# Gated mix of linear attention and a dense layer on one core: the first token tile loaded in two halves, other first loads in changed places, and parts of the first projection, the outputs and the last tile in another order

## The chip, the cores and the metric

The kernel runs on one core of one Trainium2 chip. A core has five engines with an instruction queue each: TensorE (PE) for matmuls, VectorE (DVE), ScalarE (ACT), GpSimd (POOL) and SyncE (SP), and 16 DMA engines that all queues feed. PE reads SBUF and writes PSUM; DVE and ACT bring results from PSUM back to SBUF. DMAs are issued here from SP and from ACT. The metric is the device time of the whole launch in microseconds, median over several runs.

## The reference

2048 tokens of width 512 go through two branches, mixed by a gate per token. Cut to what matters:

```
x: 2048 x 512; H = 32 heads of 16; wqkv 512 x 1536; w1 512 x 1376; w2 1376 x 512
g   = sigmoid((x * gate_w).sum(-1))
q, k, v = heads of x @ wqkv
phi(t)  = concat(softmax(t @ w_phi), softmax(-t @ w_phi))     # per head, 32 features
kv  = sum over tokens of phi(k)^T v;   z = sum over tokens of phi(k)
o   = (phi(q) @ kv) / (phi(q) @ z + 1e-6)
a   = o @ wo
b   = relu(x @ w1) @ w2
out = g * a + (1 - g) * b                                      # bf16
```

## The kernel before

The kernel is written as a graph of named tasks. Each task belongs to one engine, has the tasks it depends on, and becomes a few instructions; the dependences become semaphore waits. The order of the tasks on each engine is not computed: it is written out by hand in the table `ORDER` (`sp`, `pool`, `act`, `dve`, `pe`), and each engine runs its list strictly in that order. An engine whose next task waits holds up everything behind it. The tokens are cut into 16 tiles of 128 (number `m`) and 4 chunks of 512.

*Start.* PE first runs `warm0`: six matmuls of constants, 128x512, that need no load (L258). The first chunk of x comes as four plain loads `x00` to `x03` (one tile each, 128 KB), the first 512 columns of `w1` as four loads `w1a0` to `w1a3` (128 KB each, one per 128 rows), all at L272. ACT issues `x01`, `w1a1`, `w1a3`; SP issues `x00`, `w1a0`, `w1a2`, `x02`, `x03`, and after them `w1b` (512 KB), `wphi`, `wkT`, `w1c`, `wv`, the other chunks of x (`x1` to `x3`, transposed by the DMA, L277), `wqT` and the rest. Each tile of the first chunk is transposed on PE: `xt{m}0` and `xt{m}1`, two matmuls of 128 columns each against an identity (L350), and `xe{m}0` on ACT (L362) and `xe{m}1` on DVE (L365) bring the two halves to SBUF. `xt20` to `xt31` reuse the PSUM banks of tiles 0 and 1. Then comes the first layer, `h`: for the first tiles in pieces, `hh00` (tile 0, needs `xe00` and `w1a0`), `hh01` (tile 1, needs `xe10`), `hh1`, `hh2`, `hh3` (L405; they need `w1a1`, `w1a2`, `w1a3`), `hr0`, `hr1`, `h0_0` to `h0_3` (L411), and whole ones after that (L391), with a relu on ACT each (`rl`, L469).

*Middle.* The heads' `w_phi` is folded into the projections: `f1_0` to `f1_3` (L374) make the key matrix `WP` in four blocks of 128 rows, which `fe1_0`, `fe1_2` (DVE, L344) and `fe1_1`, `fe1_3` (ACT, L342) evict. `pr_k0` to `pr_k8` and `pr_q0` to `pr_q8` (L512) multiply one or two token tiles with it, four matmuls a tile; `pr_k0` is the first, for tiles 0 and 1. Each projection goes through an eviction on ACT (`ev`, L539), minima and maxima on DVE (`mn`, `mx`), shifts on POOL (`t1`, `t2`, L552), an exponential on ACT (`ex`, L557), sums and reciprocals on DVE (`sm`, `rc`), and a product on POOL (`nm`). Key tiles are summed on PE into `kv` (L573); query tiles are transposed by a DMA from SP (`tq`, L592).

*Outputs.* For each tile, PE makes numerators and denominators, `nd{m}_0` and `nd{m}_1` (L616); DVE divides (`rd`, `o`, L623 and L625); a DMA from SP transposes the result (`to{m}`, L630). `b{m}` is eleven matmuls of the relu layer against `w2` (L638) into one of four PSUM banks, and `a{m}` four more of the attention branch against `wo` (L644) on top of it in the same bank; a bank is free again when the tile four before has been evicted. `oe{m}` on ACT (L689) multiplies by one minus the gate into one of five output buffers, and `st{m}` (L692), issued on ACT, stores 128 KB.

*Last tile.* Tile 15 is cut into columns 0 to 352 and 352 to 512, in two banks: `b15` (L659, 22 matmuls for both parts), then `a15_0` and `a15_1` (L670). `oe15_0` runs on ACT (L677) and is stored from ACT, `oe15_1` on DVE (L680) and stored from SP (L683). SP then waits for the last stores.

Of the kernel before, what the change touches and what calls it, by code (L numbers as in the profile page):

```python
# [5 lines left out]
ACT = mybir.ActivationFunctionType  # L6
ALU = mybir.AluOpType
# [14 lines left out]
    ),  # L22
# [6 lines left out]
    "act": (  # L29
# [8 lines left out]
    ),  # L38
    "dve": (
# [10 lines left out]
    ),  # L50
# [10 lines left out]
    ),  # L61
# [87 lines left out]
def bass_gated_mix__linear_kernel_hedgehog__dense_activation_relu__prompt_kernel(  # L149
# [11 lines left out]
    x2 = A_x.rearrange("b s d -> (b s) d")  # L161
    o2 = out.rearrange("b s d -> (b s) d")
    S, D = x2.shape
    H, DH = A_w_phi.shape[0], A_w_phi.shape[1]
    DFF = B_w1.shape[1]
    P = 128
    NT = S // P
    ND = D // P
    NC = S // 512
    KT = (DFF + P - 1) // P  # L170
# [10 lines left out]
    NPH, NOM, NOT, NOS = 7, 3, 4, 5  # L181
    NDB, AB = (6, 7), (3, 4, 5, 2)
    GATE_LIMIT = 40.0
    WARM = (6 * (512,),)
    RL = 400.0
    FE = "dve"

    with ExitStack() as es:
# [5 lines left out]
        XT = sb("XT", [P, ND, S], BF16)  # L194
        HT = sb("HT", [P, KT, S], BF16)
        WT = sb("WT", [P, 2 * ND, D], BF16)
        WP = sb("WP", [P, 2, ND, D], BF16)
# [13 lines left out]
        OSB = sb("OSB", [P, NOS, D], BF16)  # L211
# [19 lines left out]
        OMG = sb("OMG", [P, NT], FP32)  # L231
        PS = E(nc.psum_tensor("PS", [P, 8, 512], FP32))
# [5 lines left out]
        def psap(off, dims):  # L238
            return ap(PS, EPS, off, dims)

        g = _Graph()
        add = g.add
# [5 lines left out]
            boost=700.0)  # L248
# [22 lines left out]
        def load(name, eng, out_, in_, deps=(), dur=0.1, lat=6.0, **how):  # L271
            add(name, eng, lambda q: q.dma_start(out=out_, in_=in_, **how), deps, dur=dur, lat=lat, dma=True,  # L272
                boost=1e4)
            after_last(name, eng)
# [12 lines left out]
        def load_x(m, eng, lat):  # L287
            load(f"x0{m}", eng, XN[:, m, :], x0r[:, m, :], dur=0.45, lat=lat)

        def load_w(j, eng, lat):  # L290
            load(f"w1a{j}", eng, W1[:, j, 0:512], w1r[:, j, 0:512], dur=0.45, lat=lat)

        load_x(0, "sp", 2.95)
        load_x(1, "act", 3.1)
        load_w(0, "sp", 3.2)
        load_w(1, "act", 3.4)
        load_w(2, "sp", 3.8)
        load_w(3, "act", 3.95)
        load_x(2, "sp", 4.0)
# [54 lines left out]
        for m in range(4):  # L354
            for n in range(2):
                add(f"xt{m}{n}", "pe", lambda q, m=m, n=n: pe_xt(q, m, n),
                    (f"x0{m}", "ident", f"xe{m - 2}{n}" if m > 1 else None), dur=0.2, boost=9000.0 - 10 * m)
            for n, eng in enumerate(("act", "dve")):
                xo = XT[:, 2 * n:2 * n + 2, m * P:(m + 1) * P]
                xi = PS[:, XB[m][n], 0:2 * P].rearrange("p (j t) -> p j t", j=2)  # L360
                if eng == "act":
                    add(f"xe{m}{n}", eng, lambda q, o=xo, i=xi: q.activation(o, i, ACT.Copy), (f"xt{m}{n}",), dur=0.35,  # L362
                        boost=9000.0 - 10 * m)
                else:
                    add(f"xe{m}{n}", eng, lambda q, o=xo, i=xi: q.tensor_copy(o, i), (f"xt{m}{n}",), dur=0.37,  # L365
                        boost=9000.0 - 10 * m)
        x0 = [f"xe{m}{n}" for m in range(4) for n in range(2)]
        xof = [x0, ["x1"], ["x2"], ["x3"]]
# [60 lines left out]
        for line in (("warm0", "xt00", "xt01", "xt10", "xt11", "hh00", "hh01", "hh1", "hh2", "xt20", "xt21", "xt30", "xt31",  # L429
                      "hh3", "hr0", "hr1"), ("xe00", "xe10", "xe20", "xe30"),  # L430
                     ("ident", "shift", "xe01", "xe11", "xe21", "xe31", "blk", "row4", "mk")):
            for a, b in zip(line, line[1:]):
                g.follow(a, b)
# [62 lines left out]
        for m in range(NT):  # L496
            def add(*a, boost=20.0 * (len(widths) * 2 - m // 2 - VLAG), **how):
                return g.add(*a, boost=boost, **how)
# [9 lines left out]

        def pe_proj(q, s, tiles):
            for n, m in enumerate(tiles):  # L510
                for j in range(ND):
                    last = q.matmul(PS[:, n, :], XT[:, j, m * P:(m + 1) * P], WP[:, s, j, :],  # L512
                                    start=(j == 0), stop=(j == ND - 1))
            return last

        jname = []
        for jn, (kind, tiles) in enumerate(jobs):
# [15 lines left out]
            def old(x, J2=two):  # L533
                return f"{x}_{J2}" if J2 else None

            add(f"pr_{J}", "pe", lambda q, s=s, tiles=tiles: pe_proj(q, s, tiles),
                [*(f"fe{s}_{j}" for j in range(ND)), *(d for m in tiles for d in xof[m // 4]),
                 *([f"ev_{before}"] if before else ["fe1_0", "fe1_1"])], dur=0.87 * w)
# [40 lines left out]
            else:  # L579
# [29 lines left out]
                for m in tiles:  # L609
# [39 lines left out]
                    if m == NT - 1:  # L649

                        hb = (ab, 0)
                        cols = [slice(0, 352), slice(352, D)]
                        last_b = f"b{m}"

                        def pe_bh(q, m=m, hb=hb, cols=cols):
                            for b, cs in zip(hb, cols):
                                for k in range(KT):
                                    r = P if k < KT - 1 else KREM
                                    last = q.matmul(PS[:, b, 0:cs.stop - cs.start], HT[0:r, k, m * P:(m + 1) * P], W2[0:r, k, cs],  # L659
                                                    start=(k == 0), stop=False)  # L660
                            return last

                        g.add(last_b, "pe", pe_bh, ("w2a", "w2b", *(f"rl{m // 4}_{k}" for k in range(KT - 1)), f"hx{m // 4}", *war,
                                                    f"ev_{J}"), dur=2.42)
                        for h2 in range(2):
                            b, cs = hb[h2], cols[h2]

# [5 lines left out]

                            add(f"a{m}_{h2}", "pe", pe_ah, (last_b, "wo", f"to{m}", f"a{m}_0" if h2 else None), dur=0.44)
                            need = (f"a{m}_{h2}", f"go{m // 4}", f"st{m - NOS}")
# [12 lines left out]
                    add(f"a{m}", "pe", pe_a, (f"b{m}", "wo", f"to{m}"), dur=0.87)  # L688
                    add(f"oe{m}", "act", lambda q, m=m, ab=ab: q.activation(  # L689
                        OSB[:, m % NOS, :], PS[:, ab, :], ACT.Copy, scale=OMG[:, m:m + 1]),  # L690
                        (f"a{m}", f"go{m // 4}", f"st{m - NOS}" if m >= NOS else None), dur=0.69)
                    add(f"st{m}", "act", lambda q, m=m: q.dma_start(  # L692
                        out=o2[m * P:(m + 1) * P, :], in_=OSB[:, m % NOS, :]), (f"oe{m}",), dur=0.5, lat=1.5, dma=True)
# [44 lines left out]
```

## Time and profile before

| | us |
|---|---|
| median of 3 runs | 150.46 (150.14 to 150.74) |
| the profiled execution | 150.59 |
| its span | 149.3 |
| PE busy | 146.3 |
| POOL busy | 109.6 |
| DVE busy | 110.9 |
| ACT busy | 91.8 |
| DMA queue of SP (q1) | 43616 packets, 13.50 MB |
| DMA queue of ACT (q10) | 2736 packets, 2.45 MB |

The profile is of one execution; its span goes from the first to the last instruction, and the time of that execution is 1.3 us longer. A group's row gives line, engine, operation, the tile written and the tiles read, then its busy time and the mean duration of one. Matmuls are pipelined: a row's duration of a single matmul is longer than the distance to the next one, so the distance between starts tells the pace. A DMA's row on SP or ACT (SPq, ACTq) is the time its issue takes; the landing comes later and is listed on its own. Idle time of an engine counts only where another engine or the end waits for it.

### The profile page before, as it was taken

The numbers are of one execution on the slowest core, as the hardware profiler recorded it, in microseconds if no ns is written. First come the engines' busy times: TensorE is split into PE (matmuls) and PEld (weight loads), VectorE is DVE, ScalarE is ACT, GpSimd is POOL, SyncE is SP. The second block draws the span as 40 slices with busy tenths as digits, with TensorE's granted clock in tenths as the row PEclk, the third lists the DMA queues.
The fourth block names the chain that finished last, engine by engine and source line by source line (L and its number), as shares of the span: only waits on it lengthen the run. The fifth ranks groups of instructions, "written<-read, shape, count | busy, mean of one in ns | idle before, by whom it ended". The sixth has DMA issues, their size and how long they took to land.

```text
span 149.3 us, 2619 instructions
## 1 busy us (share of the span) xinstructions
PE 146.3 (98%) x1009; PEld 75.9 (51%) x1009; DVE 110.9 (74%) x168; ACT 91.8 (61%) x127; POOL 109.6 (73%) x72
## 2 busy tenths in 40 slices
PE   7999999999999999999999999999999999999994
PEld 2865444444754465445444545455444444445452
DVE  2343666999796948989999997999989988534401
ACT  3374769799979775898983937175573751310151
POOL 4000399999999999999999999999999793150000
PEclk9999999999999999999999999999999999999999
DMA  5999999900030001000000094646778687656552
GB/s 144 303 234 247 171 212 211 341 27 0 7 70 0 0 4 37 0 0 4 0 0 0 2 111 104 141 103 139 121 169 190 159 212 97 156 134 159 63 156 91
DMA packets 46364, 16.11 MB, mean 108 GB/s; under 512 B 39856, under 2 KB 46352, under 8 KB 46352
## 3 DMA queue, kind: packets, MB, share of 16 engines
q1 hardware_dynamic: 43616, 13.50, 43.2%
q10 hardware_dynamic: 2736, 2.45, 5.1%
q8 instruction: 8, 0.13, 0.4%
q14 instruction: 4, 0.03, 0.1%
HBM read 4.41 MB, written 2.10 MB: 44 GB/s over the span
## 4 chain that ended last, share of the span: by engine, by line
PE 98%; DVE 0%; issue 0%
PE PS L638 24%; PE PS L391 21%; PE PS L512 19%; PE PS L492 9%; PE PS L644 9%; PE PS L573 3%; PE PS L616 3%; PE PS L399 2%; PE PS L405 2%; PE PS L258 2%; PE PS L659 2%; PE PS L411 1%; PE PS L374 1%; PE PS L350 1%; PE PS L670 1%; DVE OSB L680 0%
## 5 line engine op out<-in xcount | busy, mean ns | idle before, releaser
L552 POOL TENSOR_TENSOR TS<-PB,MX 128x1024 bf16<-128x1024 bf16 (+1 forms) x18 | 30.9, 1723 | 15.0 <-DVE MX L543 15.0
L638 PE MATMUL PS<-W,HT 128*128 128x512 bf16 (+1 forms) x165 | 38.1, 379 | 0.0
L559 DVE TENSOR_REDUCE ZB<-FT 128x128 f32<-128x2048 bf16 (+1 forms) x18 | 36.6, 2031 | 1.8 <-ACT FT L557 1.8
L557 ACT ACTIVATE FT<-TS 128x2048 bf16<-128x2048 bf16 (+1 forms) x18 | 30.9, 1718 | 8.7 <-POOL TS L552 8.5
L391 PE MATMUL PS<-XT,W 128*128 128x512 bf16 x144 | 34.7, 379 | 0.0
L552 POOL TENSOR_TENSOR TS<-MN,PB 128x1024 bf16<-128x1024 bf16 (+1 forms) x18 | 30.9, 1725 | 0.8 <-DVE MN L545 0.8
L512 PE MATMUL PS<-WP,XT 128*128 128x512 bf16 x128 | 30.6, 379 | 0.0
L566 POOL TENSOR_TENSOR FT<-FT,SC 128x2048 bf16<-128x2048 bf16 (+1 forms) x9 | 29.5, 3287 | 0.0
L469 ACT ACTIVATE HT<-PS 128x512 bf16<-128x512 f32 x40 | 22.6, 597 | 5.6 <-PE PS L391 4.6
L638 PEld LDWEIGHTS PS<-W,HT 128*128 128x128 bf16 (+1 forms) x165 | 15.5, 98 | 17.1
L689 ACT ACTIVATE OSB<-PS,OMG 128x512 bf16<-128x512 f32 x15 | 10.2, 687 | 22.4 <-PE PS L644 22.3
L543 DVE TENSOR_REDUCE MX<-PB 128x64 bf16<-128x1024 bf16 (+1 forms) x18 | 19.5, 1084 | 6.0 <-ACT PB L539 6.0
L545 DVE TENSOR_REDUCE MN<-PB 128x64 bf16<-128x1024 bf16 (+1 forms) x18 | 19.3, 1084 | 3.2 <-ACT PB L539 3.2
L391 PEld LDWEIGHTS PS<-XT,W 128*128 128x128 bf16 x144 | 13.8, 98 | 15.3
L539 ACT ACTIVATE PB<-PS 128x1024 bf16<-128x1024 f32 (+1 forms) x18 | 16.7, 927 | 7.3 <-PE PS L512 4.2
L512 PEld LDWEIGHTS PS<-WP,XT 128*128 128x128 bf16 x128 | 12.0, 98 | 13.6 <-DVE WP L344 0.4
L492 PE MATMUL PS<-WV,XT 128*128 128x512 bf16 x64 | 16.4, 379 | 0.0
L589 POOL TENSOR_TENSOR FT<-FT,SR 128x1024 bf16<-128x1024 bf16 (+1 forms) x9 | 15.7, 1739 | 0.7
L644 PE MATMUL PS<-WO,OT 128*128 128x512 bf16 x60 | 14.7, 379 | 0.0
L625 DVE SCALAR_TENSOR_TENSOR OTM<-PS,EG,RD 128x256 bf16<-128x256 f32 x32 | 13.8, 463 | 0.4 <-DVE RD L623 0.2
L623 DVE RECIPROCAL RD<-PS 128x16 f32<-128x16 f32 x32 | 6.4, 232 | 9.0 <-PE PS L616 8.8
L501 ACT ACTIVATE VS<-PS 128x512 bf16<-128x512 f32 x16 | 9.6, 602 | 4.3 <-PE PS L492 4.3
(54 smaller groups left out, 106.0 us busy)
## 6 DMA issues: line engine op xcount, KB each, us to landing
out_dram<-OSB ACTq DMA_DIRECT2D x15, 128.0 KB, 2.1
W<-in_B_w_dram SPq DMA_DIRECT2D x1, 1280.0 KB, 6.9
W<-in_B_w_dram SPq DMA_DIRECT2D x1, 512.0 KB, 4.9
WV<-in_A_wqkv_dram SPq DMA_DIRECT2D x1, 512.0 KB, 4.7
WO<-in_A_wo_dram SPq DMA_DIRECT2D x1, 512.0 KB, 7.2
FT<-in_A_x_dram SPq DMA_DIRECT2D x3, 128.0 KB, 3.8
W<-in_B_w_dram SPq DMA_DIRECT2D x1, 352.0 KB, 3.9
W<-in_B_w_dram ACTq DMA_DIRECT2D x2, 128.0 KB, 3.7
```

Source lines behind the costliest of these rows:

```text
L391: last = q.matmul(PS[:, b, :], W1[:, j, k * P:(k + 1) * P], XT[:, j, chunk(c)], start=(j == 0), stop=(j == ND - 1))
L469: add(f"rl{a}_{k}", "act", lambda q, a=a, k=k, b=b: q.activation(HT[:, k, chunk(a)], PS[:, b, :], ACT.Relu), (prev,), dur=0.6, boost=RL)
L492: last = q.matmul(PS[:, 2, :], XT[:, j, m * P:(m + 1) * P], WV[:, j, :], start=(j == 0), stop=(j == ND - 1))
L512: last = q.matmul(PS[:, n, :], XT[:, j, m * P:(m + 1) * P], WP[:, s, j, :], start=(j == 0), stop=(j == ND - 1))
L543: add(f"mx_{J}", "dve", lambda q, sl=sl, w=w, i=pbg: q.tensor_reduce(MX[:, sl, 0:w * H], i, AX.X, ALU.max), (f"ev_{J}", old("t1")), dur=0. ...
L545: add(f"mn_{J}", "dve", lambda q, sl=sl, w=w, i=pbg: q.tensor_reduce(MN[:, sl, 0:w * H], i, AX.X, ALU.min), (f"ev_{J}", old("t2")), dur=0. ...
L552: add(f"{tn}_{J}", "pool", lambda q, o3=o3, a3=a3, b3=b3: q.tensor_tensor(o3, a3, b3, ALU.subtract), (f"{'mx' if sg == 0 else 'mn'}_{J}", ...
L557: add(f"ex_{J}", "act", lambda q, fs=fs, ts=ts, w=w: q.activation(FT[:, fs, 0:w * F], TS[:, ts, 0:w * F], ACT.Exp), (f"t1_{J}", f"t2_{J}", ...
L559: add(f"sm_{J}", "dve", lambda q, fs=fs, sl=sl, w=w: q.tensor_reduce(ZB[:, sl, 0:2 * w * H], FT[:, fs, 0:w * F].rearrange("p (g d) -> p g ...
L566: add(f"nm_{J}", "pool", lambda q, f3=f3, sl=sl, w=w: q.tensor_tensor(f3, f3, SC[:, sl, 0:2 * w * H].unsqueeze(2).to_broadcast([P, 2 * w * ...
L638: last = q.matmul(PS[:, ab, :], HT[0:r, k, m * P:(m + 1) * P], W2[0:r, k, :], start=(k == 0), stop=False)
L644: last = q.matmul(PS[:, ab, :], OT[:, m % NOT, t, :], WO[:, t, :], start=False, stop=(t == ND - 1))
```

## The change

The first load is cut: rows 0 to 63 of tile 0 as `x00a` from SP, rows 64 to 127 as `x00b` from ACT. `x01` and `w1a1` follow on ACT, and `w1a3` goes from ACT to SP, in front of `x02`. `warm0` has five matmuls instead of six. For tile 0 the two evictions change engines: `xe00` on DVE, `xe01` on ACT.

```diff
-        load_x(0, "sp", 2.95)
+        for h, (part, eng) in enumerate((("a", "sp"), ("b", "act"))):
+            rows = slice(h * (P // 2), (h + 1) * (P // 2))
+            load(f"x00{part}", eng, XN[rows, 0, :], x0r[rows, 0, :], dur=0.45, lat=2.6)
+        load_w(0, "sp", 3.2)
         load_x(1, "act", 3.1)
-        load_w(0, "sp", 3.2)
+        load_w(2, "sp", 3.8)
         load_w(1, "act", 3.4)
-        load_w(2, "sp", 3.8)
-        load_w(3, "act", 3.95)
+        load_w(3, "sp", 3.95)
...
-    WARM = (6 * (512,),)
+    WARM = (5 * (512,),)
...
-                    (f"x0{m}", "ident", f"xe{m - 2}{n}" if m > 1 else None), dur=0.2, boost=9000.0 - 10 * m)
-            for n, eng in enumerate(("act", "dve")):
+                    (*((f"x0{m}",) if m else ("x00a", "x00b")), "ident", f"xe{m - 2}{n}" if m > 1 else None), dur=0.2, boost=9000.0 - 10 * m)
+            for n, eng in enumerate(("act", "dve") if m else ("dve", "act")):
```

The first key projection is cut in two tasks that follow each other on PE: `pr_k0a`, its first two matmuls, depends on `fe1_0` and `fe1_1` alone; `pr_k0`, the other six, on all four.

```diff
+            steps = [(n2, m, j) for n2, m in enumerate(tiles) for j in range(ND)]
+            if jn == 0:
+                add(f"pr_{J}a", "pe", lambda q, s=s, steps=steps[:2]: pe_proj(q, s, steps),
+                    [f"fe{s}_0", f"fe{s}_1", *xof[0]], dur=0.44)
+                steps = steps[2:]
```

In the lists of PE and ACT some output tasks change places, and the last two tiles change engines and order. On PE:

```diff
-        "... pr_q8 nd5_1 a2 nd5_0 a3 b5 nd6_0 nd6_1 b7 nd7_0 nd7_1 a4 a5 b6 nd8_1 nd8_0 ..."
+        "... pr_q8 nd5_1 a2 nd5_0 b5 a3 nd6_0 nd6_1 b6 nd7_0 nd7_1 a4 a5 b7 nd8_1 nd8_0 ..."
-        "... a11 a12 a13 a14 b15 a15_0 a15_1"
+        "... a11 a12 a13 b15_0 a14 a15_0 b15_1 a15_1"
```

On ACT `oe3` moves from behind `st0` to behind `ev_q8`; `oe14` moves to DVE, ahead of `oe15_1`, and `st14` to SP, ahead of `st15_1`. The last tile is cut at column 416 instead of 352, and `b15` becomes two tasks, `b15_0` and `b15_1`, with `a15_0` between them.

```diff
-                        cols = [slice(0, 352), slice(352, D)]
+                        cols = [slice(0, 416), slice(416, D)]
...
+                    if m < NT - 2:
+                        add(f"oe{m}", "act", lambda q, m=m, ab=ab: q.activation(
+                            OSB[:, m % NOS, :], PS[:, ab, :], ACT.Copy, scale=OMG[:, m:m + 1]), need, dur=0.69)
+                    else:
+                        add(f"oe{m}", "dve", lambda q, m=m, ab=ab: q.tensor_scalar(
+                            OSB[:, m % NOS, :], PS[:, ab, :], OMG[:, m:m + 1], None, ALU.mult), need, dur=0.75)
+                    add(f"st{m}", "act" if m < NT - 2 else "sp", lambda q, m=m: q.dma_start(
```

Everything else, lists of POOL included, stays as it was.

More of the change, by code (lines that the diff above doesn't have):

```diff
@@ L429, in bass_gated_mix__linear_kernel_hedgehog__dense_activation_relu__prompt_kernel @@
         for line in (("warm0", "xt00", "xt01", "xt10", "xt11", "hh00", "hh01", "hh1", "hh2", "xt20", "xt21", "xt30", "xt31",
-                      "hh3", "hr0", "hr1"), ("xe00", "xe10", "xe20", "xe30"),
-                     ("ident", "shift", "xe01", "xe11", "xe21", "xe31", "blk", "row4", "mk")):
+                      "hh3", "hr0", "hr1"), ("xe01", "xe10", "xe20", "xe30"),
+                     ("ident", "shift", "xe00", "xe11", "xe21", "xe31", "blk", "row4", "mk")):
             for a, b in zip(line, line[1:]):
@@ L507, in bass_gated_mix__linear_kernel_hedgehog__dense_activation_relu__prompt_kernel, with pe_proj @@
         kind_n = {"k": 0, "q": 0}
[L509 to L513, printed above, removed]
+        def pe_proj(q, s, steps):
+            for n, m, j in steps:
+                last = q.matmul(PS[:, n, :], XT[:, j, m * P:(m + 1) * P], WP[:, s, j, :],
+                                start=(j == 0), stop=(j == ND - 1))
             return last
@@ L534, in old @@
                 return f"{x}_{J2}" if J2 else None
-            add(f"pr_{J}", "pe", lambda q, s=s, tiles=tiles: pe_proj(q, s, tiles),
-                [*(f"fe{s}_{j}" for j in range(ND)), *(d for m in tiles for d in xof[m // 4]),
+            steps = [(n2, m, j) for n2, m in enumerate(tiles) for j in range(ND)]
[3 more added lines that the diff above has]
+                steps = steps[2:]
+            add(f"pr_{J}", "pe", lambda q, s=s, steps=steps: pe_proj(q, s, steps),
+                [f"pr_{J}a" if jn == 0 else None, *(f"fe{s}_{j}" for j in range(ND)), *(d for m in tiles for d in xof[m // 4]),
                  *([f"ev_{before}"] if before else ["fe1_0", "fe1_1"])], dur=0.87 * w)
@@ L651, in bass_gated_mix__linear_kernel_hedgehog__dense_activation_relu__prompt_kernel, with pe_bh @@
                         hb = (ab, 0)
-                        cols = [slice(0, 352), slice(352, D)]
-                        last_b = f"b{m}"
-                        def pe_bh(q, m=m, hb=hb, cols=cols):
-                            for b, cs in zip(hb, cols):
+                        cols = [slice(0, 416), slice(416, D)]
+                        prev = None
+                        for h2 in range(2):
+                            b, cs = hb[h2], cols[h2]
+                            def pe_bh(q, m=m, b=b, cs=cs):
                                 for k in range(KT):
@@ L660, in pe_bh @@
                                                     start=(k == 0), stop=False)
[L661 to L666, printed above, removed]
+                                return last
+                            last_b = f"b{m}_{h2}"
+                            g.add(last_b, "pe", pe_bh, ("w2a", "w2b", *(f"rl{m // 4}_{k}" for k in range(KT - 1)), f"hx{m // 4}", *war,
+                                                        f"ev_{J}", prev), dur=1.2)
+                            prev = f"a{m}_{h2}"
                             def pe_ah(q, m=m, b=b, cs=cs):
@@ L672, in pe_ah @@
                                 return last
-                            add(f"a{m}_{h2}", "pe", pe_ah, (last_b, "wo", f"to{m}", f"a{m}_0" if h2 else None), dur=0.44)
+                            add(f"a{m}_{h2}", "pe", pe_ah, (last_b, "wo", f"to{m}"), dur=0.44)
                             need = (f"a{m}_{h2}", f"go{m // 4}", f"st{m - NOS}")
@@ L688, in bass_gated_mix__linear_kernel_hedgehog__dense_activation_relu__prompt_kernel @@
                     add(f"a{m}", "pe", pe_a, (f"b{m}", "wo", f"to{m}"), dur=0.87)
[L689 to L692, printed above, removed]
+                    need = (f"a{m}", f"go{m // 4}", f"st{m - NOS}" if m >= NOS else None)
+                    if m < NT - 2:
[5 more added lines that the diff above has]
+                    add(f"st{m}", "act" if m < NT - 2 else "sp", lambda q, m=m: q.dma_start(
                         out=o2[m * P:(m + 1) * P, :], in_=OSB[:, m % NOS, :]), (f"oe{m}",), dur=0.5, lat=1.5, dma=True)
```

22 rows, old and new, of the table ORDER are left out of this document.

## The prediction

> **What bounds the kernel now.** I read the page first (shares of the engines, chain that ended last), then the timeline in stretches, in narrow windows so that each matmul shows its own start, and last the DMA issues with their time to landing. The page:
>
> ```profile
> PE 146.3 (98%) x1009; PEld 75.9 (51%) x1009; DVE 110.9 (74%) x168; ACT 91.8 (61%) x127; POOL 109.6 (73%) x72
> ...
> PE 98%; DVE 0%; issue 0%
> ```
>
> TensorE (PE) is busy all the time, and the chain that ends last is PE alone. So only three things can shorten this kernel: holes between matmuls, matmuls that run slowly, and what lies before the first and behind the last. The start, in the timeline (start, duration, engine, line, tiles; in brackets the idle time before it and who ended it):
>
> ```profile
> 0.77 2.72 PE L258 MATMUL PS<-const-bfloat16-1.0 128*128 128x512 bf16 x6 [0.77 <-PEq L723]
> 3.44 0.77 PEld L350 LDWEIGHTS PS<-IDN,FT 128*128 128x128 bf16 x8 [0.86 <-DMA FT<-in_A_x_dram]
> 3.44 1.03 PE L350 MATMUL PS<-IDN,FT 128*128 128x128 bf16 x8
> 4.31 2.49 PE L405 MATMUL PS<-XT,W 128*128 128x128 bf16 x16
> 6.64 0.61 PE L350 MATMUL PS<-IDN,FT 128*128 128x128 bf16 x8
> ```
>
> The eight transposes of 128 columns take 1.03 us at 3.44 and 0.61 at 6.64. One by one, matmuls of 512, 256 and 128 columns start 427, 213 and 107 ns apart until 6.42, and 216, 109 and 56 ns apart from there on: PE works at half speed for its first 5.65 us (the page's granted clock doesn't show this). The last warm-up matmul starts at 2.86, so it is through at 3.29; `xt00` starts at 3.44, ended by a DMA. The two loads at 0.74 (time to landing in the last column):
>
> ```profile
> FT<-in_A_x_dram ACTq DMA_DIRECT2D x1, 128.0 KB, 2.9
> FT<-in_A_x_dram SPq DMA_DIRECT2D x1, 128.0 KB, 2.7
> ```
>
> To finer digits the landings are x00 3.40, x01 3.61, and then w1a0 4.07 and w1a1 4.29. From 6.42 on there are only three holes in the PE stream over 0.05 us: 0.11 before L411 at 7.64, and these two. The first key projection:
>
> ```profile
> 12.16 0.68 DVE L344 CAST WP<-PS 128x512 bf16<-128x512 f32 x1
> 12.24 0.81 PE L391 MATMUL PS<-XT,W 128*128 128x512 bf16 x3
> 12.27 0.59 ACT L342 ACTIVATE WP<-PS 128x512 bf16<-128x512 f32 x1
> ...
> 12.97 0.13 PEld L512 LDWEIGHTS PS<-WP,XT 128*128 128x128 bf16 x2 [0.42 <-DVE WP L344]
> 13.01 0.38 PE L512 MATMUL PS<-WP,XT 128*128 128x512 bf16 x1
> ```
>
> The last L391 matmul starts at 12.67 and the next could start at 12.89; L512 starts at 13.01, as the evictions `fe1_2` and `fe1_3` end at 12.84 and 12.86: 0.12 us of hole. The other:
>
> ```profile
> 106.62 0.29 PE L616 MATMUL PS<-KVN,PHQ 128*128 128x68 bf16 x4
> 106.89 0.60 PE L644 MATMUL PS<-WO,OT 128*128 128x512 bf16 x2
> ```
>
> Four matmuls of 68 columns take 0.13 us, so L644 (`a3`) could start at 106.75: 0.15 us of hole. Its input is the transpose `to3`, issued at 102.89; the DMA issues of that moment have one line, with 3.96 us to landing, so 106.85:
>
> ```profile
> OT<-OTM SPq DMA_TRANSPOSE x1, 4.0
> ```
>
> The end:
>
> ```profile
> 146.00 1.04 PE L670 MATMUL PS<-WO,OT 128*128 128x352 bf16 x8
> 146.80 0.55 ACT L677 ACTIVATE OSB<-PS,OMG 128x352 bf16<-128x352 f32 x1 [1.74 <-PE PS L670]
> 147.08 0.38 DVE L680 TENSOR_SCALAR OSB<-PS,OMG 128x160 bf16<-128x160 f32 x1 [5.70 <-PE PS L670]
> 147.39 0.35 ACTq L683 DMA_DIRECT2D out_dram<-OSB  x1
> 147.49 0.37 SPq L683 DMA_DIRECT2D out_dram<-OSB  x1
> ```
>
> PE ends at 147.04; then `oe15_1` (0.38), its store, which lands at 149.22, and the end at 149.27.
>
> **The change, part by part.** *First key projection.* `pr_k0a` needs only `fe1_0` and `fe1_1` (ended 12.25 and 12.37), so two matmuls of 216 ns run from 12.89 to 13.32, when the other two evictions are long done: **-0.12 us**. Nothing else is queued differently.
>
> *b5 before a3.* `b5` needs the bank that `oe1` freed at 105.65, so it starts at 106.75 and runs 11 x 216 ns; `a3` comes 2.4 us later with its input there: **-0.15 us**. Late next would be `tq6`: it landed at 109.28 for `nd6` at 110.15, 0.87 spare, 0.6 after both gains. `b6` (bank free at 107.51) goes ahead of `b7`, whose bank `oe3` frees. `oe3` now stands behind `ex_q5` (its input was there at 108.38, 1.9 us long), `ge3` and `ev_q8` (0.2 and 0.6): done at about 111.7, while `b7` starts at 114.5. That cover, 2.8 us, hides the move; without it `b7` would wait us for us. Behind `oe3` on ACT stands `oe4`, which waits for `a4` until 114 anyway.
>
> *Last tile.* PE has the same 15 matmuls per part: 15 x (149 + 69) ns before, 15 x (176 + 43) after (columns at the row's rate; 97 columns of L399 start 43 ns apart, so narrow ones cost no more): nothing. `a14` and `a15_0` move behind `b15_0`, so `to14`, which landed at 142.59 for `a14` at 142.73, the tightest input of the end, gets 1.9 us more. `to15` landed at 144.16 for `a15_0`, then at 145.5: 1.4 spare. At the end `oe15_1` has 96 columns, not 160; CAST rows give 0.42 us at 256 (L365) and 0.68 at 512, so 1.0 ns a column: 0.32 for 0.38, **-0.06 us**. `oe15_0` grows to 0.61 (0.55 at 352, 0.69 at 512) but `a15_0` now ends 15 x 43 = 0.65 us before `a15_1`: hidden. `oe14` on DVE: 0.38 + 352 x 1.0 = 0.73 us, from 145.7 to 146.45; behind it waits only `oe15_1`, ready at 147.05. `st14` on SP (0.37 to issue) is through at 146.85, 0.5 before `st15_1` is ready; its 1.7 us to landing (ACT stores here: 1.7) end at about 148.2, before the 149 of `st15_1`.
>
> *First loads.* Four tiles of 128 KB landed at 3.40, 3.61, 4.07, 4.29: 0.33 us per 128 KB, from a mean of 3.50 for the first two. With the halves of x00 alone in front, x00 should land at 3.50 - 0.33 = 3.17 (bounds: 3.07, and 3.40 as now), and the second pair, now w1a0 and x01, at 3.50 + 0.33 = 3.83. Five warm-up matmuls end at 2.86, so `xt00` starts at 3.22 instead of 3.44. But PE then has four matmuls (to 3.63) and `xt10`, next in its order, waits for x01 until 3.88; before it started at 3.84. From there `xe10`, `hh01` follow as before (0.90 us behind `xt10`): `hh01` at 4.78 for 4.74. `xe00` on DVE (0.42 for ACT's 0.38) is done by 4.07, before PE is through with `xt11` at 4.30. So 0.04 us late, at half speed, and with the step to full speed unmoved at 6.42 that is 0.02 of work: **+0.02 us**. Bounds: x01 lands at 3.61 as now, `hh01` at 4.55: -0.10; x01 comes between the old w1a0 and w1a1, 4.18, `hh01` at about 5.1: +0.18. I take the middle, as bytes set the landings. w1a1 is third on ACT as w1a3 was, so the table load stays at 2.15. w1a3 on SP pushes x02, x03, w1b, wphi, wkT and all behind back by one issue, 0.47 us. Spare now: x02 0.58, x03 0.46, w1b 1.42, wkT 1.21, x1 1.72; x02 and x03 are set by bytes in front of them, which stay the same: nothing; if issue did set them, up to 0.05.
>
> One rule speaks against the split. The Trainium skill, "DMA: Bandwidth & Descriptors", section "Rules for kernel authors", says that two transfers to disjoint partition halves serialize on the same engines and are not worth it. By it x00 would land at 3.40 as before and PE would idle 0.58 us after the warm-up, not 0.36; the sum stays, as x01 sets `hh01`. In the trace x00 and x01 do share the engines (landings 0.2 apart); no row yet shows halves.
>
> **Sum:** -0.12 - 0.15 - 0.06 + 0.02 = -0.31 us. The profiled execution took 150.59 (span 149.3 and 1.3 around it), 0.13 over the median of the runs, 150.46. Its span should become 149.0, and the median **150.15 us**. What a measurement can tell from no change is about 0.5%, 0.75 us; this is within it.
>
> **The rivals.** *The clock steps up later (slower).* Place: the first 6.4 us. Nothing in the kernel's order sets the step at 6.42, so activity before it may. Before, PE stood idle 0.16 + 0.07 us in the 3.4 us up to the step; now it idles 0.36 after the warm-up and 0.25 for x01, 0.6 in all. It decides if that counts as a pause. If the 5.65 us of lead begin anew at `xt00`, the step comes at 8.87, 2.45 later; half of that is lost: +1.2 - 0.3, 151.4. For it: 2.5 us of warm-up did not bring the step by 3.3. Against: a pause was bridged before. The Trainium skill, "TensorE: Matmul & The Clock Gate", Part 1, has the gate judge free-running windows of about 3.4 us; the spacing at half and full speed agrees with its two states, and one more window would give an estimate of 1.7 us. Chance 0.11.
>
> *The first loads cost what the holes bring.* x01 at 4.18 and x03 late: +0.2 + 0.05 for +0.02, 150.4. For it: `xt10` has only 0.24 spare on x01. Against: the bytes. 0.10.
>
> *The last store is held up.* `st14`'s 128 KB leave on SP's queue ahead of `st15_1`. If they took it 0.4 us (128 KB at the 0.33 above), 150.5. Against: 0.9 us between the issues. 0.04.
>
> *The step comes earlier or the start gains more (faster).* The three runs differ by 0.6 us though the program is fixed, which a step at another time would give at half its shift. A step 0.9 us earlier in the runs measured: -0.45 more, 149.7 and below. 0.13.
>
> **How the numbers follow.** The forecast holds 0.62; with the second and third rival 0.76 lie within 0.5% (149.7 to 151.2). Faster 0.13, slower 0.11. For the range: below, 150.15 - 0.10 (start) - 0.3 (half the runs' spread), and a little of the faster case: 149.5. Above, 150.15 + 0.2 + 0.4 (store) + 0.3: 151.0. It leaves out the late step and part of the early one.
>
> **What would show it.** In the profile after: L512's first matmul 216 ns behind L391's last; `a3` behind `b5` with no wait for `to3`; `oe15_1` at 0.32 us; `xt00` near 3.2, a hole before `xt10`, `hh01` near 4.8; 256-column matmuls 109 ns apart from 6.4 on. The prediction is wrong if half speed lasts beyond 7 us, if x02 or x03 end a wait of PE, or if the 0.27 us from the two holes come back as waits on `tq` or `to` behind 107 us.

## The result, and the profile after

The changed kernel is slower by about 0.6%. The interval of the ratio lies wholly above 1, though its lower end is under the 0.5% that the prediction named as the least that can be told:

| | before | changed |
|---|---|---|
| median, us (15 runs each, in turn) | 150.30 (149.83 to 150.84) | 151.16 (150.36 to 152.22) |
| ratio, with its 95% interval | | 1.0058 [1.0039, 1.0077] |
| the profiled execution, us | 150.59 | 150.92 |
| its span | 149.3 | 149.5 |

Forecast were 150.15 (149.5 to 151.0) and no measurable change; the median lies above that range. In ratios and mean spans below, executions 1.5% above the fastest of their kernel are left out (one of e2, whose span would be +1.5 with it, and two of e8, -0.07); medians and ranges hold all.

The page after, engines and chain of waits:

```profile
PE 144.0 (96%) x991; PEld 74.6 (50%) x1008; DVE 111.6 (75%) x169; ACT 91.2 (61%) x126; POOL 109.5 (73%) x72
...
PE 94%; DMA 3%; ACTq 1%; issue 1%; DVE 0%
```

Before, the chain was PE at 98% and hardly anything else. Now 3% of the span is a DMA and 1% ACT issuing DMAs (some matmul records are missing: 991 of 1009, so the busy time is a little short). The stretch of that chain is the start (columns: start, duration, what):

```profile
0.75 0.57 ACTq L272
1.32 0.04 issue
1.36 0.85 ACTq L272
2.21 0.03 issue
2.24 4.27 DMA W<-in_B_w_dram
6.51 0.05 issue
6.55 1.05 PE PS L407 x8
```

ACT issues `x00b` for 0.57 us, `x01` for 0.85, and only then `w1a1`, which lands 4.27 us later, at 6.51; `hh1` (L407, of 256 columns) starts at 6.55. Before, `w1a1` was second on ACT, was issued at 1.18 and landed at 4.29, and `hh1` started at 5.14. What PE waits for in the whole span (total, times, longest):

```profile
PE PS L407 <- DMA W<-in_B_w_dram: 0.8, 1, 0.8
...
PE PS L352 <- issue: 0.6, 1, 0.6
PE PS L352 <- DMA FT<-in_A_x_dram: 0.4, 1, 0.4
```

Three waits, all in the first 6.6 us: for `w1a1`, for the halves of tile 0 (the row says issue, but `xt00` starts 0.09 us after the later half has landed), and for `x01`. The DMA issues near 1.3 us, with their time to landing:

```profile
FT<-in_A_x_dram ACTq DMA_DIRECT2D x1, 128.0 KB, 3.2
W<-in_B_w_dram SPq DMA_DIRECT2D x1, 128.0 KB, 2.8
FT<-in_A_x_dram SPq DMA_DIRECT2D x1, 64.0 KB, 2.2
FT<-in_A_x_dram ACTq DMA_DIRECT2D x1, 64.0 KB, 2.8
```

With the issue times: `x00a` lands at 2.98 and `x00b` at 3.54, later than the whole tile did (3.40); `x01`, issued at 1.36 for 0.74, lands at 4.57 for 3.61. `xt00` starts at 3.63 (3.44 before), `xt10` at 4.62 (3.84). The first whole matmul group of `h` (`h0_4`), here before and after:

```profile
9.40 1.89 PE L391 MATMUL PS<-XT,W 128*128 128x512 bf16 x8
```

```profile
10.41 1.67 PE L393 MATMUL PS<-XT,W 128*128 128x512 bf16 x7
```

Of the eight matmuls after, the first has no record; one distance of 0.216 earlier it started at 10.20, for 9.40. That is 0.8 us behind, although matmuls run at full speed from 4.14 on, 2.3 us earlier than in the execution profiled before.

The late parts did their work. The stretches at 13 and at 107 us in the timeline:

```profile
12.82 1.03 PE L393 MATMUL PS<-XT,W 128*128 128x512 bf16 x4
...
13.68 1.67 PE L513 MATMUL PS<-WP,XT 128*128 128x512 bf16 x7
```

```profile
107.29 0.29 PE L622 MATMUL PS<-KVN,PHQ 128*128 128x68 bf16 x4
107.42 2.54 PE L644 MATMUL PS<-W,HT 128*128 128x512 bf16 x11
110.02 0.81 PE L650 MATMUL PS<-WO,OT 128*128 128x512 bf16 x3
```

Four matmuls of 216 ns from 12.82 end at 13.68, where the key projection (L513) starts; `b5` (L644) starts 0.13 us after the first of four matmuls of 68 columns, which is all the time they take, and `a3` (L650, one of its four without a record) follows it. Both holes are gone, 0.27 us, and the end of PE is 147.56 for 147.04: 0.8 - 0.27. The end:

```profile
147.03 0.37 SPq L703 DMA_DIRECT2D out_dram<-OSB  x1
...
147.22 0.33 PE L677 MATMUL PS<-WO,OT 128*128 128x96 bf16 x4
...
147.60 0.32 DVE L687 TENSOR_SCALAR OSB<-PS,OMG 128x96 bf16<-128x96 f32 x1 [0.59 <-PE PS L677]
147.94 0.36 SPq L690 DMA_DIRECT2D out_dram<-OSB  x1
```

From PE's end to the span's end it is 1.94 us for 2.23. Of the 0.29 gained, 0.06 is `oe15_1`; the rest is the last store, whose 24 KB land 1.51 us after their issue where 40 KB took 1.73.

One part lies outside the span. The time outside it is 1.47 us in the mean of the changed kernel's executions and 1.32 for the one before, where it hardly varies (1.26 to 1.39 in the 78 executions run beside the experiments). The DMA view of the time from 149 us on shows for the changed kernel a packet that the one before doesn't have there (its last is at 140.0):

```profile
q14 instruction: 1, 0.01, 0.7%
```

A packet of 8 KB at about 150.8, on a queue that the page calls instruction.

### The profile page after: what moved, and what is told of

Its sections match the earlier page's. It is cut to its first block, busy times and chain, and to the rows that moved or that the text cites. A ratio compares the mean times of both kernels' runs of the same rounds, so it can differ in the third digit from the quotient of the medians.

```text
span 149.5 us, 2603 instructions
## 1 busy us (share of the span) xinstructions
PE 144.0 (96%) x991; PEld 74.6 (50%) x1008; DVE 111.6 (75%) x169; ACT 91.2 (61%) x126; POOL 109.5 (73%) x72
## 3 DMA queue, kind: packets, MB, share of 16 engines
q1 hardware_dynamic: 43840, 13.68, 41.8%
## 4 chain that ended last, share of the span: by engine, by line
PE 94%; DMA 3%; ACTq 1%; issue 1%; DVE 0%
PE PS L644 24%; PE PS L393 21%; PE PS L513 18%; PE PS L494 9%; PE PS L650 9%; DMA W<-in_B_w_dram 3%; PE PS L579 3%; PE PS L622 3%; PE PS L401 2%; PE PS L666 2%; PE PS L413 1%; PE PS L376 1%; PE PS L407 1%; ACTq L272 1%; PE PS L677 1%
## 5 line engine op out<-in xcount | busy, mean ns | idle before, releaser
L644 PE MATMUL PS<-W,HT 128*128 128x512 bf16 (+1 forms) x161 | 37.5, 379 | 0.2
L513 PE MATMUL PS<-WP,XT 128*128 128x512 bf16 x124 | 29.9, 379 | 0.2
L644 PEld LDWEIGHTS PS<-W,HT 128*128 128x128 bf16 (+1 forms) x165 | 15.4, 98 | 16.9
L698 ACT ACTIVATE OSB<-PS,OMG 128x512 bf16<-128x512 f32 x14 | 9.6, 686 | 21.2 <-PE PS L650 20.7
L513 PEld LDWEIGHTS PS<-WP,XT 128*128 128x128 bf16 x128 | 12.1, 98 | 13.5
L494 PE MATMUL PS<-WV,XT 128*128 128x512 bf16 x61 | 15.8, 379 | 0.2
L650 PE MATMUL PS<-WO,OT 128*128 128x512 bf16 x57 | 14.2, 378 | 0.2
```

Of the source, the lines that this page charges most:

```text
L494: last = q.matmul(PS[:, 2, :], XT[:, j, m * P:(m + 1) * P], WV[:, j, :], start=(j == 0), stop=(j == ND - 1))
L644: last = q.matmul(PS[:, ab, :], HT[0:r, k, m * P:(m + 1) * P], W2[0:r, k, :], start=(k == 0), stop=False)
L650: last = q.matmul(PS[:, ab, :], OT[:, m % NOT, t, :], WO[:, t, :], start=False, stop=(t == ND - 1))
```

## The experiments

All twelve compute the whole reference. "Span" is the mean over the executions against that of the kernel before, run in turn with it; "outside" is the mean of time less span (1.32 or 1.33 for the kernel before, beside each group of runs). For the changed kernel's row the span before is its mean time less this 1.32. "Full speed" is when the full clock begins in the profiled execution: by the trace's record of the clock where it has one, else between the two matmuls that show it by their distance.

| | median us (runs; range) | ratio to before | span | outside | full speed |
|---|---|---|---|---|---|
| changed | 151.16 (15; 150.36-152.22) | 1.0058 [1.0039, 1.0077] | +0.73 | 1.47 | 4.14 |
| e1 late parts alone | 150.05 (12; 149.59-150.47) | 0.9986 [0.9969, 1.0002] | -0.56 | 1.57 | 4.3-4.4 |
| e2 start alone | 152.19 (6; 151.39-154.11) | 1.0118 [1.0084, 1.0153] | +1.16 | 1.76 | 8.22 |
| e3 w1a1 on SP | 151.68 (6; 150.65-152.22) | 1.0089 [1.0061, 1.0118] | +0.99 | 1.50 | 8.4-8.6 |
| e4 x00 whole | 150.59 (12; 149.94-151.29) | 1.0014 [0.9994, 1.0034] | +0.04 | 1.46 | 3.80 |
| e5 e1, fewer waits | 149.84 (7; 149.41-150.37) | 0.9956 [0.9940, 0.9973] | -0.71 | 1.32 | by 3.5 |
| e6 before, more waits | 150.70 (12; 150.16-151.05) | 1.0003 [0.9987, 1.0018] | -0.08 | 1.54 | 5.93 |
| e7 e1, warm-up and evictions | 150.51 (12; 149.70-151.11) | 0.9995 [0.9977, 1.0013] | -0.47 | 1.65 | 5.67 |
| e8 halves by columns | 150.47 (12; 149.69-152.01) | 1.0000 [0.9972, 1.0027] | -0.32 | 1.52 | 3.3-4.1 |
| e9 e5, row halves on SP | 151.80 (6; 150.54-152.21) | 1.0089 [1.0060, 1.0119] | +0.78 | 1.60 | 3.60 |
| e10 e5, five warm-ups | 149.94 (12; 149.59-150.68) | 0.9964 [0.9944, 0.9985] | -0.49 | 1.31 | 6.39 |
| e11 e5, evictions exchanged | 149.96 (9; 149.34-150.30) | 0.9956 [0.9937, 0.9975] | -0.67 | 1.33 | 4.1-4.4 |
| e12 changed, seven warm-ups | 150.89 (12; 150.25-152.38) | 1.0026 [1.0001, 1.0050] | +0.20 | 1.52 | 9.9-10.0 |

Behind the letters in the texts on record stand these theories: A, the first loads cost the time, A1 by `w1a1`'s place as third on ACT, A2 by the issues of the 64-row halves, which delay all that stands behind them; C, with the shorter warm-up and the idle time the clock steps up later; D, with one instruction more on SP, code is fetched after the end.

**e1 and e2: the halves of the change.** e1 is the kernel before with the late parts (its lists for PE, ACT, DVE and SP from `pr_k0` on, the cut at 416); e2 has the start alone.

```diff
-        "... f1_3 h0_6 pr_k0 h0_7 ..."
+        "... f1_3 h0_6 pr_k0a pr_k0 h0_7 ..."
-        "... a2 nd5_0 a3 b5 nd6_0 ..."
+        "... a2 nd5_0 b5 a3 nd6_0 ..."
...
-                        cols = [slice(0, 352), slice(352, D)]
+                        cols = [slice(0, 416), slice(416, D)]
```

> Start as before (whole x00, six warm-up matmuls, old places of the loads and of xe00/xe01); first key projection, b5/a3, oe3 and the last tile as in the changed kernel. Theory A (the whole loss is in the first loads): 0.55 us faster than before, from two holes of 0.27 and 0.29 at the end, about 149.75. Rival (the loss also comes from later waits or from the last tile): no faster than before, 150.3 or more.

```diff
-        load_x(0, "sp", 2.95)
+        for h, (part, eng) in enumerate((("a", "sp"), ("b", "act"))):
+            rows = slice(h * (P // 2), (h + 1) * (P // 2))
...
-    WARM = (6 * (512,),)
+    WARM = (5 * (512,),)
```

> The other half: only the first loads, the warm-up and the engines of xe00/xe01 as in the changed kernel, all else as before. Theory A: slower than before by the measured 0.86 and the 0.55 that it does not win back, about 1.4 us, 151.7; w1a1 lands at 6 us or later and ends a wait of PE. Rival: about 150.3.

The late parts shorten the span by 0.56 us, as much as the 0.12 + 0.15 + 0.29 read above (e5, with the same late parts, has 0.71, so the match is closer than these runs can tell); the start lengthens it by 1.16. Together that is +0.60, against +0.73 for both at once. So the whole loss is the start's. e1's median, 150.05, falls short of the 149.75 expected, as its time outside the span grew by 0.25 us (e5, below). e2's expected wait didn't come, though: in its profile `w1a1` lands at 5.08, in time for `hh1` at 5.46. PE waits for the tiles alone there, 0.5 us in two waits, and stays at half speed until 8.22.

**e3: w1a1 third on SP.**

```diff
-        "x00a w1a0 w1a2 w1a3 x02 x03 ..."
+        "x00a w1a0 w1a1 w1a2 x02 x03 ..."
-        "x00b x01 w1a1 xe01 ..."
+        "x00b x01 w1a3 xe01 ..."
```

> The changed kernel with w1a1 and w1a3 in exchanged places: w1a1 third on SP, w1a3 third on ACT, halves of x00 kept. Theory A1 (the loss is w1a1 being third on ACT, needed at 5.2 us): w1a1 lands near 4.9 us as w1a2 did, no wait for it, most of the loss gone: about 150.0 to 150.2. Theory A2 (the halves delay everything, by their longer issue): w1a3 or w1a2 is late instead, still 0.5 us or more over the kernel with the old start, 150.4 to 151.

`w1a1` lands at 5.21 instead of 6.51, and the kernel is no faster; at 151.68 it is above both forecasts. A1 falls: with that wait gone the one for `x01`, behind the same long issues, is 0.73 us.

```profile
0.75 1.46 ACTq L272 DMA_DIRECT2D FT<-in_A_x_dram  x2
...
4.56 0.61 PE L352 MATMUL PS<-IDN,FT 128*128 128x128 bf16 x4 [0.73 <-DMA FT<-in_A_x_dram]
```

**e4: tile 0 whole on SP, the rest as changed.**

```diff
-        for h, (part, eng) in enumerate((("a", "sp"), ("b", "act"))):
-            rows = slice(h * (P // 2), (h + 1) * (P // 2))
-            load(f"x00{part}", eng, XN[rows, 0, :], x0r[rows, 0, :], dur=0.45, lat=2.6)
+        load_x(0, "sp", 2.95)
```

> The changed kernel with x00 whole on SP again; so x01 and w1a1 are first and second on ACT, w1a3 fourth on SP, five warm-up matmuls, xe00 on DVE. Theory A1 and A2 alike: w1a1 lands at 4.3 us as before, no wait for it, about 149.7 to 149.9. Theory C (fewer warm-up matmuls and the idle time behind them put off the step to full speed): full speed comes later than 7 us and the time stays over 150.5. The issues of the first loads take 0.40 us again if the 64-row shape made them 0.58.

The span comes back by 0.69 of the 0.73 us. Of the forecasts, A is right that the wait for `w1a1` goes (it lands at 4.30), but had the time at 149.7 to 149.9; C had the time, over 150.5, but not the reason, as full speed comes at 3.80. The timeline of its start, and what PE then waits for:

```profile
0.74 0.40 SPq L272 DMA_DIRECT2D FT<-in_A_x_dram  x1
0.75 0.41 ACTq L272 DMA_DIRECT2D FT<-in_A_x_dram  x1
...
1.18 0.46 ACTq L272 DMA_DIRECT2D W<-in_B_w_dram  x1
```

```profile
PE PS L350 <- DMA FT<-in_A_x_dram: 0.5, 1, 0.5
PE PS L391 <- DMA W<-in_B_w_dram: 0.3, 1, 0.3
PE PS L374 <- DMA WT<-in_A_wqkv_dram: 0.3, 1, 0.3
```

The loads of 128 rows issue in 0.40 to 0.46 us, and `x00` and `x01` land at 3.16 and 3.33. What stays against e1 (0.04 + 0.56 = 0.60 us of span) shows in the waits: `x03`, `w1b` and `wkT`, the loads that `w1a3` pushes back on SP, land at 6.81, 9.50 and 11.65 (before: 6.41, 7.98 and 9.92), and PE, at full speed from 3.80, waits for all three. That the place of `w1a3` makes them so late isn't shown: in e8, with the same order and full speed as early, `w1b` and `wkT` land at 8.12 and 10.28, and PE waits for neither.

**e5 and e6: SP's waits at the end.** SP waits for the last stores. e5 is e1 without the waits for `st9` and `st10`: `oe14` and `oe15_0` wait for these already, as they write the same output buffers. e6 is the kernel before with three more, for `st6` to `st8`.

```diff
-        for m in range(NT - NOS - 2, NT - 1):
+        for m in range(NT - NOS, NT - 1):
```

> e1 (start as before, late parts as changed) without SP's last two waits for st9 and st10, which the order of the other stores implies. Theory D: the changed kernels have one more DMA on SP, and SP's instructions then reach into one more 8 KB block of code, fetched after the last store has landed; that lengthens what lies outside the span from 1.32 to 1.47 to 1.77 us. With two instructions fewer on SP the last 8 KB fetch is gone, the time outside the span is 1.32 again, the median 149.85. Rival: the time outside the span varies for another reason; it stays at 1.5, the median at 150.05.

```diff
-        for m in range(NT - NOS - 2, NT - 1):
+        for m in range(NT - NOS - 5, NT - 1):
```

> The kernel before with three more waits at the end of SP's list, for stores that landed long ago. Theory D: an 8 KB fetch appears behind the span, the time outside it goes from 1.32 to about 1.5, the median from 150.3 to 150.5, the span stays. Rival: no fetch, no difference.

Outside the span e5 takes 1.32 us in the mean (1.27 to 1.35 in its seven executions), e1 1.57, e6 1.54. In the profiles, the packet of the instruction queue behind the end is there in e1 and in e6, here the row of e6 from 149 us on:

```profile
q14 instruction: 1, 0.01, 1.0%
```

and nothing moves in e5 from 149 us on. So the length of SP's list decides whether the packet can come: shown by both edits. It doesn't come each time. Of the fourteen profiled executions, eight have it and take 1.42 to 1.71 us outside the span, six don't and take 1.32 to 1.35; two of the six are e7 and e8, whose lists are as long as e1's or longer and whose means are 1.65 and 1.52. That the fetch itself takes the time is inferred from this. e6's median moved by less than can be told. e5 has the lowest median of the study and is faster than the kernel before and the changed one; e10 and e11 can't be told from it.

**e7, e10, e11: warm-up and evictions.** e7 is e1 with five warm-ups and `xe00` and `xe01` exchanged; e10 and e11 put these on e5 one at a time.

```diff
-    WARM = (6 * (512,),)
+    WARM = (5 * (512,),)
...
-            for n, eng in enumerate(("act", "dve")):
+            for n, eng in enumerate(("act", "dve") if m else ("dve", "act")):
```

> e1 with five warm-up matmuls and xe00 on DVE, xe01 on ACT; loads in their old places. Theory: of what e4 (150.59) still loses against e1 (150.05), the place of w1a3 on SP, in front of x02, w1b and wkT, is the cause, and this kernel is as fast as e1, 150.05. Rival: the missing warm-up matmul or the exchange of engines is the cause, 150.5.

> e5 with five warm-up matmuls instead of six, nothing else. e7 lost about 0.24 us of span against e5 with this and the exchange of xe00 and xe01. If the missing matmul is the cause (less activity, full speed later): 150.1 beside an e5 of 149.85. If not: as e5.

> e5 with xe00 on DVE and xe01 on ACT, six warm-up matmuls. If the exchange is the cause of e7's 0.24 us: 150.1. If not: as e5, 149.85.

e7's median is the rival's 150.5, but in span it is only 0.09 us behind e1, which is nothing, and 0.24 behind e5. Against e5's -0.71, the exchange is worth +0.05 us of span and five warm-ups +0.22: the first is nothing, the second a small loss at the edge of what these runs can tell; e10's median, 149.94, is nearer to e5's than to the 150.1 named for a loss.

**e8 and e9: which halves, on which queue.** e8 is the changed kernel with tile 0 cut by columns (128 rows of 512 bytes each); e9 is e5 with the row halves, both on SP.

```diff
-            rows = slice(h * (P // 2), (h + 1) * (P // 2))
-            load(f"x00{part}", eng, XN[rows, 0, :], x0r[rows, 0, :], dur=0.45, lat=2.6)
+            cs = slice(h * (D // 2), (h + 1) * (D // 2))
+            load(f"x00{part}", eng, XN[:, 0, cs], x0r[:, 0, cs], dur=0.45, lat=2.6)
```

> The changed kernel with tile 0 cut by columns (128 rows of 512 bytes from each queue) instead of by rows (64 rows of 1024 bytes). Theory A2 in the form that the 64-row shape makes the issues long (0.58 us, and 0.85 for one behind): issues of 0.40 again, x01 lands near 3.9 instead of 4.5, and the time comes to e4's, 150.6. Rival (two DMAs for one tile are the cause, whatever their shape): x01 lands at 4.3 or later, 151.2.

```diff
-        "x00 w1a0 w1a2 x02 x03 w1b ..."
+        "x00a x00b w1a0 w1a2 x02 x03 w1b ..."
...
+            load(f"x00{part}", "sp", XN[rows, 0, :], x0r[rows, 0, :], dur=0.45, lat=2.6)
```

> e5 with tile 0 cut by rows, both halves on SP one behind the other; ACT and everything else as in e5. If the 64-row shape is what makes an issue long, x00a and x00b take 0.58 us each on SP while ACT's 128-row issues stay at 0.41 to 0.46, and SP's loads behind them come 0.75 us later: 0.3 to 0.6 us slower than e5, span about 149.0. If halves cost only when two queues share a tile, all issues take 0.40, and the loss is one issue, span about 148.7.

The same bytes as column halves issue in 0.40 us each; with `x01` behind, ACT is through 0.89 us after its first issue, for 1.46 in the changed kernel. In the timeline of e8:

```profile
0.74 0.40 SPq L272 DMA_DIRECT2D FT<-in_A_x_dram  x1
0.74 0.89 ACTq L272 DMA_DIRECT2D FT<-in_A_x_dram  x2
...
1.66 0.45 ACTq L272 DMA_DIRECT2D W<-in_B_w_dram  x1
```

and in that of e9, where only SP issues row halves:

```profile
0.73 1.21 SPq L272 DMA_DIRECT2D FT<-in_A_x_dram  x2
0.75 0.38 ACTq L272 DMA_DIRECT2D FT<-in_A_x_dram  x1
1.15 0.94 ACTq L272 DMA_DIRECT2D W<-in_B_w_dram  x2
...
4.75 0.61 PE L352 MATMUL PS<-IDN,FT 128*128 128x128 bf16 x8 [1.25 <-issue]
```

The long issue goes with the shape and stays on the queue that has it: in e9 ACT issues as ever, and SP takes 0.58 and 0.57 for the halves and 0.58 for `w1a0` behind them. A2 holds by e8: nothing but the shape of the halves differs from the changed kernel, `x01` lands at 4.00 instead of 4.57, and the span is 1.05 us shorter. e9 is 1.50 us longer than e5, far above the 0.3 to 0.6 expected, and this isn't the price of the issues alone: the second half stands second on SP there, lands at 4.66, and PE waits 1.25 us for it. e8 still isn't faster than before, and 4 of its 12 executions lie at 151.45 to 152.01, the other 8 at 149.69 to 150.63; why is open (below).

**e12: the changed kernel with seven warm-ups.**

```diff
-    WARM = (5 * (512,),)
+    WARM = (7 * (512,),)
```

> The changed kernel with seven warm-up matmuls instead of five (they end at 3.72, about when xt00 can start). Theory C (PE's idle time behind the warm-up puts the step to full speed off by a stretch in part of the executions; with row halves it came after 8 us in two of three profiles): the late executions go, median about 150.5 and no run over 151.5. Rival (only the loads count): 151.1 as the changed kernel, with the same spread.

The longest of its twelve executions, 152.38, is the profiled one, and here the clock steps up last:

```profile
5.26 3.02 PE L407 MATMUL PS<-XT,W 128*128 128x128 bf16 x16
8.07 1.06 PE L352 MATMUL PS<-IDN,FT 128*128 128x128 bf16 x8
```

Eight transposes at 8.07 still take 1.06 us, half speed, and matmuls stay there until 9.9. So more warm-up doesn't exclude a late step, and C falls in that form. e12's mean span is 0.53 below the changed kernel's, but the intervals of the two ratios overlap, so that the warm-up helps on average isn't shown.

## Why the prediction was wrong

*First loads: the step that failed.* Its words were "I take the middle, as bytes set the landings", and +0.02 us with bounds from -0.10 to +0.18. Measured is +1.16 to +1.44 of span (e2 alone; the changed kernel less e1 or e5). Three things were left out of that step.

- The issue of a half was taken to cost what a whole load costs, 0.40 to 0.46. It took 0.55 to 0.58 in all five profiles with row halves, and the issue behind it 0.56 to 0.85 (the table load on ACT came at 2.72, not at 2.15). So `x01` went out at 1.36 and landed at 4.57, not at 3.83, and its upper bound, 4.18, was exceeded too. `xt00` started at 3.63 and `hh01` at 5.38, for about 3.2 and 4.8 forecast. Nor was tile 0 there sooner: in the four profiles with a half on each queue the later half lands at 3.15 to 3.54, 3.28 in the mean, and a whole first tile in eight profiles at 3.08 to 3.42, 3.29 in the mean. `x01` lands at 4.13 to 4.81 in the four and at 3.26 to 3.61 in the eight. By e4 the split is worth about 0.7 us.
- "w1a1 is third on ACT as w1a3 was, so the table load stays": the text looked at what stands behind `w1a1` and not at who waits for it. `w1a3`, third on ACT, had landed at 5.89, and `hh1` needs `w1a1` at 5.14; that row alone gave a wait of 0.75. Here the third load of ACT, issued at 1.67 before and at 2.24 after, with its time to landing:

```profile
W<-in_B_w_dram ACTq DMA_DIRECT2D x1, 128.0 KB, 4.2
```

```profile
W<-in_B_w_dram ACTq DMA_DIRECT2D x1, 128.0 KB, 4.3
```

So `w1a1`, third there now, landed at 6.51 and ended the longest wait of PE (in e12 it landed at 6.35, in e2 at 5.08 and without a wait). e3 shows that curing this alone cures nothing, since the halves stand ahead of everything.
- `w1a3` on SP "pushes ... back by one issue, 0.47 us ... nothing". The spare times, 0.46 to 1.42, were read in an execution whose clock stepped up at 6.42. In e4 it stepped up at 3.80, PE came to each load earlier, and three waits appeared. An early step brings a wait with the old order too: in e5, at full speed by 3.5, PE waits 0.6 us for a part of `w1`. Taking e10's 0.22 for the warm-up from the 0.60 that e4 keeps against e1 leaves about 0.4 for the place of `w1a3`; it wasn't tried alone.

The Trainium skill, "DMA: Bandwidth & Descriptors", section "Rules for kernel authors", advises one 128-partition transfer in place of two on disjoint partition halves. The outcome agrees: e4 is faster than the changed kernel, and row halves landed no sooner than whole tiles (3.28 and 3.29 us). The reason it gives, that halves serialize on the same engines, doesn't cover the price paid here, the long issues; and halves by columns, in the one profile that has them, landed at 2.81 and 2.99, before any whole tile.

*First key projection, b5 before a3.* Right: both holes gone, with their 0.12 and 0.15 us, and neither came back as a wait for `tq` or `to`; the list of PE's waits has none behind 6.6 us.

*Last tile.* Right in kind, too small: -0.29 for -0.06. `oe15_1` took the 0.32 us forecast; the store was taken to land as before, and a store of 24 KB landed 0.22 sooner than one of 40 KB. The feared hold-up by `st14` didn't occur.

*Around the span.* "1.3 around it" was taken as fixed. It was 1.47: SP's list had grown by `w1a3` and `st14`, and either alone is enough to bring the code fetch behind the end (e2 and e1; e5 and e6 show that the length counts).

The sum, against the +0.87 us in the mean: late parts -0.56 for -0.33, start about +1.3 for +0.02, outside +0.15 for 0.

*The rivals.* "The first loads cost what the holes bring" had the place, and with 0.25 us a fifth of the price. "The clock steps up later" named 8.87; the profiled executions of e2, e3 and e12 stepped up at 8.2 to 10.0, that of the changed kernel at 4.14. Late steps thus occur with row halves (three profiles of five; the latest of the nine others is 6.42), and cost: at half speed, 2.5 us more (8.9, the mean of the three, less 6.4) are about 1.2 us of work, an estimate. That the halves cause them isn't shown. How often they come in the changed kernel isn't known, as only one execution of each kernel has a profile; how much of e4's 0.69 is the issues themselves and how much such steps stays open. So does what makes the upper four executions of e8. Of the signs named for being wrong, none shows in the changed kernel's profile (half speed ends at 4.14, and neither `x02` nor `x03` nor anything behind 107 us ends a wait); the wait for `w1a1` was not among them.

## What to carry to other kernels

Ahead of the first matmul, count issues and their order on each queue, not bytes: for every load that changes place, read the row of the one that stood there before and ask who needs it when. By e8, cut a tile by columns rather than by rows if it must be cut, and look at the issue's length in a profile first. Slack read in one execution at half speed is gone when the next one steps up earlier.

## What the runs showed that was not expected

- The issue of a 64-row load: 0.55 to 0.58 us for 64 KB, against 0.38 to 0.41 for the first load on a queue with 128 rows, of 64 or of 128 KB; with a cost for the next issue on that queue (0.56 to 0.85). Why wasn't found.
- The step to full speed falls anywhere from about 3.5 to 10.0 us, in kernels in which PE starts at 0.77 us in the same way. The Trainium skill, "TensorE: Matmul & The Clock Gate", Part 1, explains a spread by free-running windows of 3.4 us, and gives ±500 ns for it; that the step moves from run to run agrees, the size doesn't. In the eight traces that record it, the stretch at full clock lasts 143.36 or 146.77 us, 42 or 43 times 3.413, which agrees with such windows; why the step is a window or two later in some executions is open.
- Code fetched on the instruction queue behind the last instruction: 1.32 to 1.35 us outside the span without it, 1.42 to 1.71 with it, in fourteen profiled executions.
